# Expert stage of an attention and mixture-of-experts kernel: VectorE turns x from slot 4 and h from slot 5 on, and its turn of h goes first

## The chip, the cores and the metric

The kernel runs on one core of one Trainium2 chip. The metric is the device time of one execution in microseconds. Before the change it is 828.74 us, the median of three runs (827.8 to 831.38).

## The reference

```
scores = q k^T / 8, masked by blocks of 64, softmax, times v     # 8 batches, 8 heads, 576 x 64
x = attention output, 4608 tokens x 512
expert_idx = argmax of the cosine of x and 8 expert vectors; gate_w = its softmax value
for e in 8 experts:
    h = relu(x[mask] @ w1[e])                 # 512 -> 1024
    out[mask] = gate_w[mask] * (h @ w2[e])    # 1024 -> 512
```

All of it is float32. Each token goes to one expert only, and how many each expert gets depends on the data.

## The kernel before

The attention stage writes each token's row of x into a DRAM table, sorted by expert. The expert stage, about the second half of the time, then works in *slots* of 128 tokens of one expert. A table on the chip (`tab`) says for each slot which rows it takes, and whether it is the first of its expert. Two slots are done early, while the attention stage ends; the others are numbered from 0, and each has a `first(g)` and a `second(g)` in the program.

**One slot.** Layer 1 (`layer1`, in `first`) multiplies x by w1, layer 2 (`layer2`, in `second`) multiplies h by w2. To keep float32 precision each operand is split into a high part and a low part, and each product is three TensorE matmuls (`mm3`, L932): 24 matmuls per layer and slot. The high part is a cast on ScalarE, the low part a subtraction on VectorE. TensorE contracts over partitions, so x and h must first be *turned* (transposed).

**Two ways to turn.** TensorE can do it: `xt` turns x with four transposes (L911), `ht` turns h with eight (L963). Or VectorE does it: its transpose works inside blocks of 32 x 32 (`turned`, L860), and the blocks are brought to their places by DMA. For x this is done while it is fetched: `fetch` issues four DMAs in place of one (L851 in place of L848). For h it needs a trip through DRAM: `h_store` (L882, on ScalarE's DMA queue, two halves) writes the relu's result, `h_load` (L890, on GpSimd's queue, four DMAs into the single buffer `hq`) reads it back by blocks, `h_turn` is the pair of VectorE transposes into PSUM, and `h_in` makes the high parts (ScalarE, L869) and low parts (VectorE, L867).

**What sets which way.** `TURN` is the first slot whose h VectorE turns, `XTURN` the number from which x goes to VectorE (x of slot `XTURN + 1` is the first). `LAG` is `TURN - 2`: up to slot LAG layer 2 of slot g - 1 follows layer 1 of slot g; slot LAG + 1 has no layer 2; from then on layer 2 of slot g - 2 follows layer 1 of slot g, so that the trip of h has the time of a slot.

**Weights.** w1 and w2 of an expert are loaded raw (`load_raw`, SyncE's DMA queue, into a single buffer per layer) and split into the half of a ring that the expert before last used: per layer four pieces of 128 x 1024, each a cast on ScalarE (L714) and a subtraction on VectorE (L718). The pieces are placed by the slot G at which an expert begins, two at a time, and stand under an `If` on the slot's flag (`next_weights`): layer 1's in `second(G - 1)` and `first(G)`; layer 2's in `first(G + 1)` and `second(G + 1)`, or one slot later once the lag is two (`seconds`). When pieces are split, the raw weights of the next expert but one are loaded into their place. In slots where no expert begins, the branch skips them.

**Order.** The program is written out by hand, and every engine runs its own instructions in that order. So the lines of `second` are the order on VectorE and on ScalarE: x's turn and its parts, then pieces of weights, then (before the change) the turn of h; `h_load` and `fetch` on GpSimd's queue; layer 2; at the end the parts of h. `last` finishes the last slots and is not touched.

Of the kernel before, what the change touches and what calls it, by code (L numbers as in the profile page):

```python
# [34 lines left out]
def kernel(  # L35
# [755 lines left out]
        nc.vector.tensor_copy(tab.rearrange("p f s -> p (f s)"), tp[0:1, 0:NFL * n])  # L791

    AHEAD = 4
    TURN = 12
    LAG = TURN - 2
    XTURN = 6

    def rotate(pool, name, n, shape, dt):
        sets[name] = [pool.tile(shape, dt, name=f"{name}{i}") for i in range(n)]
# [18 lines left out]
    def next_weights(g, i, cs=range(NPC)):  # L818
        if g >= NSLOT:
            return  # L820
        sl = slots[g]
        if g == 0:
            for c in cs:
                split_hi(i, c, 1)
                split_lo(i, c, 1)
            load_raw(i, 2, cs)
            return
        body = sl["body", i]
        for en, fn in (("act", split_hi), ("dve", split_lo)):
            with tc.If(sl["to", en] != 0):  # L830
                to = sl["to", en] & 1
                for c in cs:
                    ins = fn(i, c, to)
                    for en2, c2, o in body:
                        if en2 != en and c2 != c:
                            tc.declare_no_dep(ins.ins, o.ins, reason="other columns of the ring")
                    body.append((en, c, ins))
        with tc.If(sl["first_sp"] != 0):
            load_raw(i, sl["en2"], cs)

    def fetch(g, eng=nc.gpsimd, et=mybir.EngineType.Pool):
        slots[g]["xg"] = xg = take("xg")
        slots[g]["gate"] = take("gate")
        w = DM // GQ
        r = nc.values_load(tab[0:1, 5, g:g + 1], min_val=0, max_val=(E * RE - 1) * P, engines=[et])
        rows = xs[bass.ds(r, P), :]
        if g <= XTURN:
            eng.dma_start(xg, rows[:, 0:DM])  # L848
        else:
            for q_ in range(GQ):  # L850
                eng.dma_start(xg[32 * q_:32 * q_ + 32].rearrange("j (g w) -> j g w", g=GQ),  # L851
                                    rows[:, q_ * w:(q_ + 1) * w].rearrange("(g j) w -> j g w", g=GQ))
        eng.dma_start(slots[g]["gate"], rows[:, DM:DM + TW])
# [4 lines left out]
    def turned(rows, cs, nk):  # L858
        out = take("px")
        nc.vector.transpose(out.rearrange("p (g c j) -> p g c j", g=GQ, j=32),  # L860
                            rows.rearrange("p (g i c) -> p g c i", g=GQ, c=nk)[:, :, cs, :])
        return out.rearrange("p (g c j) -> p c g j", g=GQ, j=32)
# [8 lines left out]
    def x_turn(g):  # L871
        slots[g]["xt"] = turned(slots[g]["xg"], slice(0, NC1), NC1)

    def x_in(g):
        slots[g]["xT"] = take("xh"), take("xl")
        part(0, *slots[g]["xT"], slots[g]["xt"])

    def x_low(g):
        part(1, *slots[g]["xT"], slots[g]["xt"])

    def h_store(g, f):
        nc.scalar.dma_start(hrows[g % 2][f // 512], slots[g]["h"][:, f:f + 512])  # L882

    def h_load(g):

        slots[g]["hq"] = hq = take("hq")
        w = DF // GQ
        for q_ in range(GQ):
            rows = hrows[g % 2][q_ // 2]
            nc.gpsimd.dma_start(hq[32 * q_:32 * q_ + 32].rearrange("j (g x) -> j g x", g=GQ),  # L890
                                rows[:, q_ % 2 * w:(q_ % 2 + 1) * w].rearrange("(g j) x -> j g x", g=GQ))

    def h_turn(g):
        slots[g]["ht"] = [turned(slots[g]["hq"], slice(f, f + 4), NF) for f in range(0, NF, 4)]

    def h_in(g, us=(0, 1)):
        if 0 in us:
            slots[g]["hT"] = take("hh"), take("hl")
        hh, hl = slots[g]["hT"]
        for u in us:  # L900
            for w in range(2):
                part(w, hh[:, 4 * u:4 * u + 4], hl[:, 4 * u:4 * u + 4], slots[g]["ht"][u])

    def xt(g, px=None):
        xt_copy(g, xt_pe(g, px))
# [36 lines left out]
    def layer1(g, out=True):  # L942
# [4 lines left out]
        for f in range(0, DF, 512):  # L947
# [3 lines left out]
            slots[g]["h"] = h  # L951
            if out and g >= TURN:
                h_store(g, f)

    def ht(g, fs=(0, 4), pts=None):
        for f in fs:
            ht_copy(g, f, ht_pe(g, f, None if pts is None else pts[f // 4]))
# [28 lines left out]
    def layer2(g, cs=None, y=None):  # L986
        if cs is None or 0 in cs:
            slots[g]["py"] = take("py")
        py = slots[g]["py"]
        mm3(g, 1, py, slots[g]["hT"], DM, NF, 0, cs)  # L990
        if cs is None or NF - 1 in cs:
            give(g, py, slots[g]["gate"][:, 0:1], token(slots[g]["gate"]), y)
# [52 lines left out]
    for u in range(EARLY):  # L1045
        g = len(slots)
# [121 lines left out]
    def seconds(g):  # L1168
        return g - 1 if g < LAG + 2 else g - 2
# [15 lines left out]
    def second(g):  # L1185

        if g >= NU - 1:
            for f in range(0, DF, 512):
                h_store(g, f)
        if g < XTURN:  # L1190
            xt(g + 1)
        if g >= XTURN - 1 and g + 2 < NSLOT:
            x_turn(g + 2)
            x_in(g + 2)
            x_low(g + 2)
        if g != LAG + 2:
            next_weights(seconds(g), 1, (2, 3))
        if g == 1:
            next_weights(1, 0)
        next_weights(g + 1, 0, (0, 1))  # L1200
        if g > TURN:
            h_turn(g - 1)
        if g >= TURN:
            h_load(g)
        if g <= LAG:
            layer2(g - 1)
        elif g > LAG + 1:
            layer2(g - 2, y=slots[g + 2]["xg"] if g + 2 < NSLOT else None)
        if LAG + 1 < g <= TURN:
            ht(g - 1)  # L1210
        if g + AHEAD < NSLOT:
            fetch(g + AHEAD)
        if g > TURN:
            h_in(g - 1)
# [15 lines left out]
    def rest(g):  # L1230

        if g + 1 == NSLOT:
            last(g)
            return
        used = nc.values_load(tab[0:1, 3, g + 1:g + 2], min_val=0, max_val=1)
        with tc.If(used != 0) as c:  # L1236
            second(g)
            first(g + 1)
            rest(g + 1)
        with c.Else():  # L1240
            last(g)

    for g in range(1, NU):
        first(g)
        if g < NU - 1:
            second(g)
# [49 lines left out]
```

## Time and profile before

| | |
|---|---|
| median of three runs | 828.74 us (827.8 to 831.38) |
| the profiled execution | 831.03 us, span 829.4 us |
| granted clock of TensorE, mean | 0.982 |
| TensorE busy | 800.4 us, 97% of the span |
| VectorE, ScalarE, GpSimd busy | 529.9, 409.9, 421.4 us |
| moved by DMA | 121.17 MB, mean 146 GB/s |

The expert stage proper, where `first` and `second` alternate, goes from about 422 us of the span to its end. An instruction's row gives its line, its engine and the tiles that it writes and reads. A bracket tells how long the engine was idle before it and what ended that: another engine's result, a DMA's landing, or the engine's own queue of branches (a name with a q).

### The profile page before, as it was taken

How to read it: one execution, taken by the hardware profiler on the slowest of the kernel's cores; microseconds unless marked ns; L12 is line 12 of the kernel's file. 1: busy time of each engine (PE TensorE's matmuls, PEld its weight loads, DVE VectorE, ACT ScalarE, POOL GpSimd, SP SyncE). 2: the span in 40 equal slices, each digit the busy share in tenths (PEclk: the TensorE clock that was granted, in tenths of full speed). 3: DMA queues.
4: the chain of work that ended last, by engine and by line, in shares of the span. 5: the costliest groups of instructions: out<-in, count | busy, mean ns of one | idle time of the engine just before them, and what ended most of it. 6: DMA issues, size and time to landing. Idle time of an engine off the chain costs nothing. (4 is left out here: it accounts for less than half of the span.)

```text
span 829.4 us, 21361 instructions
## 1 busy us (share of the span) xinstructions
PE 800.4 (97%) x6575; PEld 630.6 (76%) x6575; DVE 529.9 (64%) x981; ACT 409.9 (49%) x733; POOL 421.4 (51%) x554
## 2 busy tenths in 40 slices
PE   6999999999999999987999999999999999999996
PEld 3777777777777777765778888888888888888875
DVE  5677878787878787846843346655766554665441
ACT  2444646575746565665544446554544333543332
POOL 4366665756565656552421322335565555455551
PEclk7899999999999999988999999999999999999999
DMA  4766454545444454363475425767868544454441
GB/s 65 145 153 140 88 140 76 140 86 145 90 120 100 109 119 90 104 239 129 152 286 171 155 66 166 242 194 205 248 219 259 155 137 149 130 154 154 150 136 42
DMA packets 147124, 121.17 MB, mean 146 GB/s; under 512 B 123102, under 2 KB 123422, under 8 KB 145436
## 3 DMA queue, kind: packets, MB, share of 16 engines
q1 hardware_dynamic: 122752, 62.33, 29.9%
q0 software_dynamic: 17584, 44.98, 18.2%
q10 hardware_dynamic: 6636, 12.09, 4.0%
q8 instruction: 63, 1.03, 0.6%
q14 instruction: 89, 0.73, 0.3%
HBM read 84.90 MB, written 35.27 MB: 145 GB/s over the span
## 5 line engine op out<-in xcount | busy, mean ns | idle before, releaser
L365 ACT ACTIVATE pT<-psp 128x576 f32<-128x576 f32 (+2 forms) x192 | 112.5, 614 | 44.7 <-PE psp L235 43.8
L347 POOL TENSOR_TENSOR pS<-pT 128x896 f32<-128x896 f32 (+1 forms) x32 | 66.6, 2080 | 104.8 <-ACT pT L365 104.8
L235 PE MATMUL psp<-hi 64*128 64x64 f32 (+6 forms) x768 | 115.1, 336 | 3.9 <-DVE nmx L316 1.7
L316 DVE TENSOR_REDUCE nmx<-psp 128x2 f32<-128x1024 f32 (+3 forms) x128 | 103.3, 823 | 20.4 <-PE psp L235 15.8
L932 PE MATMUL py<-ring_h,hh 128*128 (+1 forms) x288 | 112.7, 391 | 0.4 <-issue 0.4
L932 PE MATMUL py<-ring_h,hl 128*128 (+1 forms) x288 | 112.3, 390 | 0.0
L932 PE MATMUL py<-ring_l,hh 128*128 (+1 forms) x288 | 112.1, 389 | 0.0
L932 PE MATMUL ph<-ring_h,xh 128*128 x280 | 110.0, 393 | 0.4 <-issue 0.4
L383 PE MATMUL psb<-pT,vo 128*64 128x448 f32 (+4 forms) x768 | 105.3, 411 | 4.5 <-DVE lgh L431 4.1
L932 PE MATMUL ph<-ring_h,xl 128*128 x280 | 109.1, 390 | 0.0
L932 PE MATMUL ph<-ring_l,xh 128*128 x280 | 109.0, 389 | 0.0
L235 PEld LDWEIGHTS psp<-hi 64*128 64x128 f32 (+1 forms) x768 | 71.7, 184 | 42.0 <-DVE lo L301 9.8
L890 POOL DMA_DIRECT2D hq<-hrows x92 | 50.3, 553 | 99.2 <-DVE px L860 87.3
L347 POOL TENSOR_TENSOR pS<-pS,pT 128x640 f32<-128x640 f32 (+3 forms) x96 | 96.0, 1000 | 9.0 <-ACT pT L365 1.7
L718 DVE TENSOR_TENSOR ring_l<-raw,ring_h 128x1024 f32 (+1 forms) x64 | 78.1, 1233 | 17.7 <-ACT ring_h L714 11.2
L950 ACT ACTIVATE h<-ph 128x512 f32<-128x512 f32 x70 | 41.8, 597 | 83.5 <-PE ph L932 74.2
L383 PEld LDWEIGHTS psb<-pT,vo 128*64 128x64 f32 x768 | 49.2, 142 | 42.9 <-issue 25.6
L399 ACT COPY so<-psb 128x896 f32<-128x896 f32 x32 | 29.0, 907 | 103.7 <-PE psb L397 103.7
L301 DVE TENSOR_TENSOR lo<-psp,hi 128x640 fp32r<-128x640 f32 x64 | 48.5, 758 | 34.5 <-ACT hi L299 32.0
L714 ACT CAST ring_h<-raw 128x1024 f32 (+1 forms) x64 | 66.5, 1053 | 7.2 <-ACTq L830 4.2
L860 DVE STREAM_TRANSPOSE px<-hq 128x512 f32<-128x512 f32 x46 | 50.7, 1146 | 19.6 <-DMA hq<-hrows 7.9
L932 PEld LDWEIGHTS py<-ring_h,hh 128*128 128x128 f32 x288 | 54.1, 188 | 11.8 <-issue 0.8
(243 smaller groups left out, 1654.5 us busy)
## 6 DMA issues: line engine op xcount, KB each, us to landing
raw<-in_moe_w_dram SPq DMA_DIRECT2D x40, 512.0 KB
raw<-in_moe_w_dram SPq DMA_DIRECT2D x12, 1024.0 KB
hrows<-h ACTq DMA_DIRECT2D x46, 256.0 KB
hq<-hrows POOLq DMA_DIRECT2D x92, 128.0 KB, 3.1
nat<-in_q_dram SPq DMA_DIRECT2D x64, 144.0 KB
nat<-in_k_dram SPq DMA_DIRECT2D x64, 144.0 KB
vo<-in_v_dram SPq DMA_DIRECT2D x64, 128.0 KB
xg<-xs POOLq DMA_DIRECT2D x64, 64.0 KB, 3.2
```

Source lines behind the costliest of these rows:

```text
L235: nc.tensor.matmul(out(hh), lhsT(hd[hh]), rhs(hd[hh]), start=start, stop=stop)
L301: nc.vector.tensor_tensor(lo_[i][:, :, cs], src, hi_[i][:, :, cs].bitcast(F32), op=ALU.subtract)
L316: nc.vector.tensor_reduce(m[:, :, u], mx[:, :, 0:P * u], axis=AX.X, op=ALU.max, negate=True)
L347: eng.tensor_tensor(o, pT[0:r, hs, P:S] if t == 1 else o, pT[0:r, hs, off[t]:off[t] + w], op=ALU.add)
L365: nc.scalar.activation(pT[0:r, :, o:o + c1 - c0], st[0:r, :, x:x + c1 - c0], AF.Exp, scale=scale)
L383: nc.tensor.matmul(ob[hh * D:(hh + 1) * D, c0:c1], a[:, t, hh, :], pTs[0][:, hh, o:o + c1 - c0], start=(t == 0), stop=(c0 == OB or t == NJ ...
L714: return nc.scalar.copy(piece(ring_h, to, c, half), raw[i][:, c * CW:(c + 1) * CW])
L718: return eng.tensor_tensor(piece(ring_l, to, c, half), raw[i][:, c * CW:(c + 1) * CW], piece(ring_h, to, c, half).bitcast(F32), op=ALU.sub ...
L860: nc.vector.transpose(out.rearrange("p (g c j) -> p g c j", g=GQ, j=32), rows.rearrange("p (g i c) -> p g c i", g=GQ, c=nk)[:, :, cs, :])
L890: nc.gpsimd.dma_start(hq[32 * q_:32 * q_ + 32].rearrange("j (g x) -> j g x", g=GQ), rows[:, q_ % 2 * w:(q_ % 2 + 1) * w].rearrange("(g j) ...
L932: m = nc.tensor.matmul(out, a[:, c, :], w, start=(c == 0 and w is wh and a is sh), stop=(c == nk - 1 and a is sl_))
L950: nc.scalar.activation(h[:, f:f + 512], ph, AF.Relu)
```

## The change

`TURN` goes from 12 to 5 and `XTURN` from 6 to 3; with TURN, LAG goes from 10 to 3. In `second`, the call of `h_turn` moves from behind the weights' pieces to the front, ahead of x's turn.

```diff
     AHEAD = 4
-    TURN = 12
+    TURN = 5
     LAG = TURN - 2
-    XTURN = 6
+    XTURN = 3
...
         if g >= NU - 1:
             for f in range(0, DF, 512):
                 h_store(g, f)
+        if g > TURN:
+            h_turn(g - 1)
         if g < XTURN:
             xt(g + 1)
         if g >= XTURN - 1 and g + 2 < NSLOT:
...
         if g == 1:
             next_weights(1, 0)
         next_weights(g + 1, 0, (0, 1))
-        if g > TURN:
-            h_turn(g - 1)
         if g >= TURN:
             h_load(g)
```

VectorE's instructions in the second half of slot 13, before the change (px are PSUM tiles of turned blocks, xg a slot's x, hq the h that was loaded back, ring_h and ring_l the weights' parts, 6409 layer 2's and 6178 layer 1's):

```order
L860 STREAM_TRANSPOSE px_6687<-xg_6415 128x512
...
L867 TENSOR_TENSOR xl_6189<-px_6687,xh_6187 128x512
...
L718 TENSOR_TENSOR ring_l_6409<-raw_6179,ring_h_6408 128x1024
...
L718 TENSOR_TENSOR ring_l_6178<-raw_109,ring_h_6177 128x1024
...
L860 STREAM_TRANSPOSE px_6685<-hq_6413 128x512
L860 STREAM_TRANSPOSE px_6686<-hq_6413 128x512
L867 TENSOR_TENSOR hl_6253<-px_6685,hh_6252 128x512
L867 TENSOR_TENSOR hl_6253<-px_6686,hh_6252 128x512
```

The same place with the change, again VectorE in the second half of slot 13:

```order
L860 STREAM_TRANSPOSE px_6690<-hq_6413 128x512
L860 STREAM_TRANSPOSE px_6688<-hq_6413 128x512
L860 STREAM_TRANSPOSE px_6689<-xg_6415 128x512
...
L867 TENSOR_TENSOR xl_6189<-px_6689,xh_6187 128x512
...
L718 TENSOR_TENSOR ring_l_6409<-raw_6179,ring_h_6408 128x1024
...
L718 TENSOR_TENSOR ring_l_6178<-raw_109,ring_h_6177 128x1024
...
L867 TENSOR_TENSOR hl_6253<-px_6690,hh_6252 128x512
L867 TENSOR_TENSOR hl_6253<-px_6688,hh_6252 128x512
```

The pair of turns of hq has moved ahead of x's turn, its low part and the pieces of both rings; the low parts of h stay last. From slot 6 on VectorE has this order in every slot.

TensorE where slot 7 begins, before the change (py is layer 2's sum, ph layer 1's):

```order
L932 MATMUL py_6688<-ring_h_6408,hl_6253 128x512
L963 MATMUL px_6687<-ident,h_6250 128x128 x4
L963 MATMUL px_6685<-ident,h_6250 128x128 x4
L943 TENSOR_LOAD tab
...
L932 MATMUL ph_6683<-ring_h_6177,xh_6187 128x512
```

TensorE at the same place with the change:

```order
L932 MATMUL py_6692<-ring_h_6408,hl_6253 128x512
L943 TENSOR_LOAD tab
L943 ISA x2
L932 ISA
L932 MATMUL ph_6686<-ring_h_6177,xh_6187 128x512
```

The eight transposes of h between the two layers are gone.

## Rows read from the trace of the kernel before

In a timeline the columns are start, length, engine, line, operation, tiles written and read, number, and in brackets the idle time ahead with what ended it.

**Rows 1.** The page's first part, TensorE's line: busy us (share), instructions.

```profile
PE 800.4 (97%) x6575; PEld 630.6 (76%) x6575; DVE 529.9 (64%) x981; ACT 409.9 (49%) x733; POOL 421.4 (51%) x554
```

**Rows 2.** Two stretches: us, PE, PEld, DVE, ACT, POOL busy, clock, DMA, GB/s.

```profile
492.00:560.00 68.00, 68.00 (x325) 57.10 (x324) 41.14 (x42) 38.87 (x54) 22.50 (x35) 1.00 0.63 197
574.00:642.00 68.00, 68.00 (x302) 56.31 (x301) 47.34 (x49) 33.44 (x49) 38.89 (x62) 1.00 0.76 239
```

**Rows 3.** TensorE's timeline: layer starts in slots 5, 6, 7, 13, 14, 15, 17.

```profile
471.15 0.48 PE L932 MATMUL ph<-ring_h,xh 128*128 x1
...
483.50 0.48 PE L932 MATMUL ph<-ring_h,xh 128*128 x1
...
495.31 0.48 PE L932 MATMUL ph<-ring_h,xh 128*128 x1
...
565.37 0.39 PE L932 MATMUL py<-ring_h,hh 128*128 x1
...
570.81 0.39 PE L932 MATMUL ph<-ring_h,xh 128*128 x1
...
581.69 0.39 PE L932 MATMUL ph<-ring_h,xh 128*128 x1
...
608.89 0.39 PE L932 MATMUL py<-ring_h,hh 128*128 x1
```

**Rows 4.** VectorE's timeline around slot 14.

```profile
572.21 1.29 DVE L867 TENSOR_TENSOR hl<-px,hh 128x512 fp32r<-128x512 f32 x2 [1.50 <-ACT hh L869]
574.02 2.56 DVE L718 TENSOR_TENSOR ring_l<-raw,ring_h 128x1024 f32 x2 [0.53 <-ACT ring_h L714]
576.91 1.11 DVE L860 STREAM_TRANSPOSE px<-xg 128x512 f32<-128x512 f32 x1 [0.33 <-DMA ex<-xs]
578.67 0.69 DVE L867 TENSOR_TENSOR xl<-px,xh 128x512 fp32r<-128x512 f32 x1 [0.65 <-ACT xh L869]
579.62 2.55 DVE L718 TENSOR_TENSOR ring_l<-raw,ring_h 128x1024 f32 x2 [0.25 <-ACT ring_h L714]
582.87 2.20 DVE L860 STREAM_TRANSPOSE px<-hq 128x512 f32<-128x512 f32 x2 [0.69 <-DMA gate<-xs]
584.96 1.45 DVE L867 TENSOR_TENSOR hl<-px,hh 128x512 fp32r<-128x512 f32 x2
587.23 1.10 DVE L860 STREAM_TRANSPOSE px<-ex 128x512 f32<-128x512 f32 x1 [0.81 <-DVEq L830]
```

**Rows 5.** ScalarE's timeline at the start of slot 14.

```profile
571.01 0.69 ACT L979 ACTIVATE xg<-py,gate 128x512 f32<-128x512 f32 x1 [3.86 <-PE py L932]
571.60 1.07 ACT L869 CAST hh<-px 128x512 fp32r<-128x512 f32 x2
572.54 2.16 ACT L714 CAST ring_h<-raw 128x1024 f32 x2
```

**Rows 6.** Stores and loads of h, in order of time, from four engines' timelines.

```profile
555.88 0.33 ACTq L882 DMA_DIRECT2D hrows<-h  x1
...
560.12 2.19 POOL L890 DMA_DIRECT2D hq<-hrows  x4 [6.54 <-DMA hrows<-h]
...
599.18 1.65 SPq L136 DMA_DIRECT2D raw<-in_moe_w_dram  x2
...
600.41 0.36 ACTq L882 DMA_DIRECT2D hrows<-h  x1
...
609.66 1.09 POOL L890 DMA_DIRECT2D hq<-hrows  x2 [2.71 <-DMA hrows<-h]
...
613.53 2.22 DVE L860 STREAM_TRANSPOSE px<-hq 128x512 f32<-128x512 f32 x2 [2.13 <-DMA hq<-hrows]
```

**Rows 7.** Splits on VectorE, 492 to 560 us: busy, mean ns | idle.

```profile
L718 DVE TENSOR_TENSOR ring_l<-raw,ring_h 128x1024 f32 x20 | 24.4, 1226 | 5.8 <-ACT ring_h L714 2.2 <-DMA raw<-in_moe_w_dram 1.9 <-DVE ring_l L718 0.5
...
514.93 5.01 DVE L718 TENSOR_TENSOR ring_l<-raw,ring_h 128x1024 f32 x4 [0.25 <-ACT ring_h L714]
```

**Rows 8.** Tile hq, the h loaded back: time from issue to landing.

```profile
DMA to landing us min/median/max: 2.8/3.1/4.9
```

## The prediction

> **What bounds the kernel now.** I read the page first. TensorE is busy for 97% of the span [rows 1]. A share over the whole span says little about one stage, so the next view was the busy time by stage: in both stretches of the expert stage TensorE works 68.00 of 68.00 us [rows 2]. It waits for nothing there, so whatever is taken off TensorE shortens the kernel, and whatever makes it wait lengthens it, one for one. The third view was TensorE's timeline, where one reads the step from slot to slot; the last were the timelines of VectorE, ScalarE and GpSimd in single slots, to see how late the turned h may come.
>
> **What goes from TensorE.** The start of layer 1 in slots 5, 6, 7, 14 and 15 stands in [rows 3]. A slot with both turns on TensorE takes 483.50 - 471.15 = 12.35 us, one that turns h alone 495.31 - 483.50 = 11.81, one with none 581.69 - 570.81 = 10.88. So a turn of x costs 0.54 us and a turn of h 0.93. Slots 5 to 11 lose the turn of h and slots 4 to 6 that of x: 7 x 0.93 + 3 x 0.54 = 8.1 us. The slot in which layer 2 is skipped to gain the longer lag moves from 11 to 4; the number of layers stays, so this costs nothing. ScalarE's and VectorE's high and low parts of h and x stay as many as before.
>
> **What is added, and what hides it.** Per slot VectorE gets a pair of h turns, 2.20 us, and in three slots an x turn, 1.11 us [rows 4]. In 492 to 560 us it was busy 41 of 68 us [rows 2], so seven pairs (15.4 us) fit as a mean. ScalarE gets two stores of h per slot, GpSimd four loads of 0.55 us, and x of slots 4 to 6 comes in four pieces in place of one; GpSimd was busy 22.5 of 68 us there, and it waits for layer 2's result anyway. I cost these issues at nothing. If that cover went, the whole of four issues, 2.2 us, would come into the trip of h priced below.
>
> **What becomes tight.** h of slot g-1 must be cut into its parts before layer 2 of that slot starts. I count from the moment when TensorE enters the second half of slot g (its layer 1 is done); 10.9 us later it needs the high parts, and after two matmuls (5.44 us for 24, so 0.45) the first low part. The budget is 11.3 us plus whatever TensorE already lost in this slot. Let the pair of h turns start at L. Then the changed order puts on VectorE: the pair 2.2, the turn of x 1.1, the high part of x on ScalarE 0.65, its low part 0.7, then the weights' low parts, then the low parts of h [rows 4]. ScalarE is in order too, and its high part of x stands ahead of layer 2's result (0.6) and of the high parts of h (0.6 each) [rows 5]. So the wait for h is now also a wait for x and weights, on both engines. From L to the end of the first low part of h:
> - no weights in the half: 2.2 + 1.1 + 0.6 + 0.6 + 0.6 + 0.7 = 5.8 us;
> - a pair of weight pieces: 2.2 + 1.1 + 0.65 + 0.7 + 0.25 + 2.55 + 0.7 (branch) + 0.7 = 8.9 us;
> - two pairs, by the row with four pieces, 5.01 us [rows 7]: 10.6 us.
> Another 0.6 us later VectorE is free. From there to the next pair of turns it needs 0.8 us (584.96 + 1.45 to 587.23), with a pair of pieces in the next first half 3.4 (572.21 + 1.29 to 576.91) [rows 4], with two pairs 3.4 + 2.8 = 6.2.
>
> **The trip of h through memory.** Here I bound from both sides. Quiet: a store issued at 555.88 let the load go at 560.12, 4.24 us. Behind weights: the store of 600.41 was issued beside two loads of raw weights (from 599.18 on), and the load of its half started only at 609.66, 9.25 us [rows 6]. The turn behind it began at 613.53, 4.6 us after the second half of slot 17 (608.89 [rows 3]). So L is 4.6 where the slot before split a pair in its first half. The other bound is from the load of 560.12: its last issue starts at 561.8 and lands a median 3.1 us later [rows 8], at 564.9, 0.5 us ahead of slot 13's second half (565.37 [rows 3]); that step still had a turn of h on TensorE, so without it L is 0.4. Before the change such lateness cost nothing, since x and the weights went ahead of the turn.
>
> On this the Trainium skill has a rule ("DMA: Bandwidth & Descriptors", section "Queues, rings and completion order"): a DMA engine goes round the queues that hold work and drains a whole packet from one before it turns to the next. By it a store would share with every load in flight, not only with one issued just ahead of it. The rows above agree for one store. By the rows the sum is the one below, by the rule it is nearer to the slow rival.
>
> **The sum, slot by slot.** VectorE's 20 pieces in 492 to 560 us [rows 7], those of [rows 4] and the loads of 599.18 [rows 6] fit experts that begin at slots 7, 9, 12 and 16. With the longer lag the second-layer pieces come one slot later, so slots 6 to 18 get (pairs in first half, second half): 6 (0,1), 7 (1,0), 8 (0,1), 9 (2,1), 10 (0,0), 11 (1,2), 12 (1,0), 13 (0,0), 14 (1,1), 15 (0,1), 16 (1,0), 17 (0,0), 18 (1,1).
> - Slot 8: after slot 7's pair L is 4.6; I add 1.8, the step from the median landing of 3.1 us to the longest, 4.9 [rows 8], as this stretch had 197 GB/s already [rows 2] and gets 1 MB of h in every 10.9 us on top, some 96 GB/s, above the 239 of the stretch from which the 4.6 is. 6.4 + 8.9 = 15.3, over the budget by 4.0.
> - Slot 9: VectorE ends slot 8 at 15.9; + 6.2 - 10.9 gives L = 11.2; + 8.9 = 20.1 against 11.3 + 4.0: 4.8.
> - Slot 10: its step is 10.9 + 4.0, so L = 20.7 + 0.8 - 14.9 = 6.6, and 12.4 against 11.3 + 4.8. Slot 11: L = 13.0 + 3.4 - 15.7 = 0.7, 11.3 against 11.3. Slots 12 and 13, with L = 4.6: 10.4. No wait.
> - Slot 14: L = 11.0 + 3.4 - 10.9 = 3.5, 12.4: 1.1. Slot 15: L = 4.6, 13.5 against 12.4: 1.1. Slots 16 to 19 end inside their budgets.
> Together 11.0 us of new waits against 8.1 saved: +2.9 us. The profiled execution took 831.03 us (span 829.4 and what lies around it), 2.3 above the median of the runs, 828.74. So 833.9 for a like execution and 831.6 on the runs' scale.
>
> **Rivals.** *The trips stay quiet.* If the loads of weights, which the new order also moves, miss the stores, L is 0.4 wherever the trip sets it. Slot 8 then ends at 9.9, and only slot 9 is over: L = 9.9 + 6.2 - 10.9 = 5.2, 14.1, a wait of 2.8. Total -8.1 + 2.8 = -5.3: 823.4 us. For it: the seven turns fit as a mean, and the store of 555.88 came through in 4.24 us. Against it: the stretch that gets the turns is the one with four experts' weights in it.
>
> *The trips get slower still.* If the load back of h is held up as the store was, by some 4 us more, L becomes 8.6 after each first half with a pair. It decides from L = 11.3 - 5.8 = 5.5 in a slot without splits and from 2.4 in one with a pair. By the same steps slots 8, 9, 12, 14, 15, 18 and 19 are over by 6.2, 4.8, 3.1, 2.0, 4.2, 0.9 and 2.2: 23.4, so +15.3: 844.0 us. For it: the 9.25 us row, and that each wait of VectorE now holds the splits back, and with them later loads. Against it: each wait of TensorE gives the memory time.
>
> *The removed turns were free.* Then neither gain nor more than the waits: 840. The fixed steps of [rows 3] and TensorE's 68.00 of 68.00 speak against it; I give it almost nothing.
>
> **Chances.** Forecast 0.43 (own range 826.5 to 837), quiet trips 0.26, slower trips 0.23, the rest in between. A measurement can tell about 0.5%, 4.1 us. Below 824.6 lie most of the quiet case and a little of the forecast's, 0.26; above 832.9 lie the slow one and the upper part of the forecast's range, 0.41; between, 0.33. The range goes from 822.0, a little under the quiet case, to 843.0, just short of the slow one.
>
> **What would show it.** TensorE's turns of h fall from 12 slots to 5 ahead of the last slots, and the step of a free slot from 11.81 to 10.88. The waits, if I am right, stand before layer 2's matmuls, ended by VectorE's low part or ScalarE's high part of h, mostly 10 to 30 us after slot 7, and VectorE waits for the h that was loaded. If TensorE is dense in slots 8 to 16, the quiet case holds. If it waits in slots 12, 15, 18 and 19 too, the slow one does. I am wrong altogether if the waits are of another kind: a bank of PSUM not free, raw weights not landed, or x late for layer 1.

## The result, and the profile after

The changed kernel takes 841.17 us (median of 4 runs, 841.08 to 843.02), the kernel before in the same comparison 829.83 (4 runs): ratio 1.014, 95% interval 1.0117 to 1.0163. The profiled execution took 841.15 us, its span is 839.5 (before 829.4). This and the other ratios below leave out executions over 1.5% above their kernel's fastest, of which only number 3 (four of ten) and the kernel before beside numbers 1 to 4 (three of 31) had any.

TensorE's share and two stretches, which answer to [rows 1] and [rows 2], in the same columns:

```profile
PE 799.4 (95%) x6507; PEld 624.3 (74%) x6507; DVE 544.4 (65%) x998; ACT 407.9 (49%) x733; POOL 442.5 (53%) x591
```

```profile
492.00:560.00 68.00, 62.34 (x260) 49.90 (x259) 45.67 (x48) 33.89 (x48) 32.10 (x52) 0.95 0.74 233
574.00:642.00 68.00, 64.17 (x269) 50.65 (x268) 45.42 (x48) 32.03 (x47) 36.56 (x61) 0.97 0.70 214
...
660.00:814.00 154.00, 154.00 (x681) 127.55 (x680) 83.02 (x94) 57.85 (x96) 87.88 (x145) 1.00 0.48 150
541.00:550.00 9.00, 8.32 (x25) 6.58 (x26) 6.89 (x7) 4.71 (x8) 4.96 (x8) 0.64 0.67 194
540.70:541.60 0.90, 0.00 (x0) 0.00 (x0) 0.00 (x0) 0.90 (x3) 0.32 (x2) 0.50 0.85 250
```

TensorE was dense in both stretches before; now it loses 5.7 and 3.8 us in them, and its clock is below 1.00. Behind 660 us it is dense again. The loss lies at layer 2 in the second halves of slots 10 to 19; the prediction counts such a wait to the slot before, in whose second half that h is turned, and so does this text: slots 9 to 18. What TensorE waited for there (engine, line, releaser: us, times, longest):

```profile
PE py L932 <- ACT hh L869: 8.5, 6, 3.7
PE py L932 <- DVE hl L867: 1.4, 4, 0.7
```

Only the two parts of h, always ahead of layer 2. TensorE's timeline, first where slots 7 to 9 begin (to be compared with [rows 3]), then at the longest wait and at one behind which the clock stays up:

```profile
487.09 0.39 PE L932 MATMUL ph<-ring_h,xh 128*128 x1
...
497.97 0.39 PE L932 MATMUL ph<-ring_h,xh 128*128 x1
...
508.85 0.39 PE L932 MATMUL ph<-ring_h,xh 128*128 x1
...
541.68 0.79 PE L932 MATMUL py<-ring_h,hh 128*128 x1 [3.67 <-ACT hh L869]
...
542.70 0.63 PE L932 MATMUL py<-ring_h,hl 128*128 x1
543.12 0.63 PE L932 MATMUL py<-ring_h,hh 128*128 x1
...
628.27 0.50 PE L932 MATMUL py<-ring_h,hh 128*128 x1 [0.84 <-ACT hh L869]
628.61 0.40 PE L932 MATMUL py<-ring_l,hh 128*128 x1
```

A slot without a wait now takes 10.88 us: the turns are gone as foreseen. The wait of 3.67 us has a tail: up to 547.5 us the matmuls come every 0.43 us instead of every 0.23. The row of 541 to 550 us above gives the granted clock there as 0.64; TensorE has it at the lower of its two levels, 1.2 GHz, for 6.83 us, and for 3.41 us again behind the wait of 2.01 us at 581. The 6.83 us begin at 540.67, a us before the wait ends: in the row of 540.70 to 541.60 the clock is 0.50 and TensorE has no matmul. Where the clock stays at 1.00, the first matmuls behind a wait still come every 0.33 to 0.39 us (628.27 to 628.61).

Why the h of slot 9 was late in slot 10 is read from four engines. VectorE:

```profile
504.92 2.18 DVE L860 STREAM_TRANSPOSE px<-hq 128x512 f32<-128x512 f32 x2 [4.26 <-DMA hq<-hrows]
507.01 1.06 DVE L860 STREAM_TRANSPOSE px<-ex 128x512 f32<-128x512 f32 x1
...
519.05 2.18 DVE L860 STREAM_TRANSPOSE px<-hq 128x512 f32<-128x512 f32 x2
...
536.19 2.17 DVE L860 STREAM_TRANSPOSE px<-hq 128x512 f32<-128x512 f32 x2 [8.33 <-DMA ex<-xs]
538.28 1.04 DVE L860 STREAM_TRANSPOSE px<-xg 128x512 f32<-128x512 f32 x1
```

ScalarE:

```profile
503.61 0.60 ACT L950 ACTIVATE h<-ph 128x512 f32<-128x512 f32 x1 [2.12 <-PE ph L932]
504.24 0.33 ACTq L882 DMA_DIRECT2D hrows<-h  x1
508.10 0.59 ACT L869 CAST xh<-px 128x512 fp32r<-128x512 f32 x1 [3.89 <-DVE px L860]
...
512.66 4.18 ACT L714 CAST ring_h<-raw 128x1024 f32 x4
516.74 0.59 ACT L950 ACTIVATE h<-ph 128x512 f32<-128x512 f32 x1
517.37 0.34 ACTq L882 DMA_DIRECT2D hrows<-h  x1
...
518.38 0.45 ACTq L882 DMA_DIRECT2D hrows<-h  x1
...
539.36 0.59 ACT L869 CAST xh<-px 128x512 fp32r<-128x512 f32 x1 [10.60 <-DVE px L860]
540.46 0.69 ACT L979 ACTIVATE xg<-py,gate 128x512 f32<-128x512 f32 x1 [0.52 <-ACTq L830]
541.05 1.06 ACT L869 CAST hh<-px 128x512 fp32r<-128x512 f32 x2
```

GpSimd, which loads h back:

```profile
525.76 1.10 POOL L890 DMA_DIRECT2D hq<-hrows  x2 [9.32 <-DMA hrows<-h]
527.68 1.09 POOL L890 DMA_DIRECT2D hq<-hrows  x2 [0.83 <-DMA hrows<-h]
```

SyncE, which loads the raw weights:

```profile
511.55 8.05 SPq L136 DMA_DIRECT2D raw<-in_moe_w_dram  x5
...
526.48 0.33 SPq L136 DMA_DIRECT2D raw<-in_moe_w_dram  x1
```

Read it as a circle. At 504.92 the h of slot 7 comes to VectorE, which has waited 4.26 us for it. The turn of x stands behind it, and ScalarE's cast of x waits for that (3.89 us). So ScalarE is late for its next work in order, two weight pieces, y, the high parts of h and four more pieces, and the relu of slot 9 comes at 516.74 and 517.75: layer 1 of slot 9 had ended at 514.45, and the second store leaves at 518.38, 3.9 us later, where a free ScalarE needs 0.67 (503.57 to 504.24). Not all of that is the cast's: in number 5 below, where x is not held, the same store still leaves 1.85 us after layer 1, behind the four pieces. The stores now also meet five weight loads; GpSimd gets the landed halves 8.4 and 9.3 us after the issues (quiet it was 4.24 [rows 6]). The load back is late as well: its last part, issued at 528.23 after the weight load of 526.48, lands after 7.7 us, at 535.97. So the h of slot 9 is turned only at 536.19, after 8.33 us of waiting (the releaser named there is a neighbour in time; the wait is for hq), and x's cast is held 10.60 us, and with it the next relu. In the 16 slots from 470 to 653 us the second store leaves 3.0 us after the end of layer 1 as a mean, 7.9 at most (the issue's row less the end of the last ph row); before, 1.05 and 2.2.

Over the whole stage the load back is no slower than before in the median (2.8 us, before 3.1 [rows 8]), but its longest has gone from 4.9 to 7.7, and that one is slot 10's. Tile hq's line, over the stage and for 527 to 529 us alone:

```profile
DMA to landing us min/median/max: 2.5/2.8/7.7
...
DMA to landing us min/median/max: 7.7/7.7/7.7
```

### The profile page after: what moved, and what is told of

It reads as the page before. It is cut to its first block, busy times and chain, and to the rows that moved or that the text cites. A ratio compares the mean times of both kernels' runs of the same rounds, so it can differ in the third digit from the quotient of the medians.

```text
span 839.5 us, 21306 instructions
## 1 busy us (share of the span) xinstructions
PE 799.4 (95%) x6507; PEld 624.3 (74%) x6507; DVE 544.4 (65%) x998; ACT 407.9 (49%) x733; POOL 442.5 (53%) x591
## 5 line engine op out<-in xcount | busy, mean ns | idle before, releaser
L890 POOL DMA_DIRECT2D hq<-hrows x120 | 65.8, 553 | 118.1 <-DMA hrows<-h 57.8
L932 PE MATMUL py<-ring_h,hh 128*128 (+1 forms) x288 | 115.0, 399 | 8.5 <-ACT hh L869 8.5
L316 DVE TENSOR_REDUCE nmx<-psp 128x2 f32<-128x1024 f32 (+3 forms) x128 | 103.2, 823 | 21.6 <-PE psp L235 18.7
L932 PE MATMUL py<-ring_h,hl 128*128 (+1 forms) x288 | 114.6, 398 | 1.4 <-DVE hl L867 1.4
L932 PE MATMUL py<-ring_l,hh 128*128 (+1 forms) x288 | 113.9, 396 | 0.0
L235 PEld LDWEIGHTS psp<-hi 64*128 64x128 f32 (+1 forms) x768 | 72.3, 185 | 42.8 <-DVE lo L301 10.1
L860 DVE STREAM_TRANSPOSE px<-hq 128x512 f32<-128x512 f32 x60 | 65.9, 1144 | 56.6 <-DMA hq<-hrows 33.4
L718 DVE TENSOR_TENSOR ring_l<-raw,ring_h 128x1024 f32 (+1 forms) x64 | 78.1, 1234 | 17.3 <-ACT ring_h L714 12.4
L950 ACT ACTIVATE h<-ph 128x512 f32<-128x512 f32 x70 | 41.8, 598 | 69.7 <-PE ph L932 44.4
L867 DVE TENSOR_TENSOR hl<-px,hh 128x512 fp32r<-128x512 f32 x60 | 38.7, 685 | 55.9 <-ACT hh L869 55.0
```

The source lines that it names most:

```text
L235: nc.tensor.matmul(out(hh), lhsT(hd[hh]), rhs(hd[hh]), start=start, stop=stop)
L316: nc.vector.tensor_reduce(m[:, :, u], mx[:, :, 0:P * u], axis=AX.X, op=ALU.max, negate=True)
L718: return eng.tensor_tensor(piece(ring_l, to, c, half), raw[i][:, c * CW:(c + 1) * CW], piece(ring_h, to, c, half).bitcast(F32), op=ALU.sub ...
L867: nc.vector.tensor_tensor(lo, src, hi.bitcast(F32), op=ALU.subtract)
L932: m = nc.tensor.matmul(out, a[:, c, :], w, start=(c == 0 and w is wh and a is sh), stop=(c == nk - 1 and a is sl_))
L950: nc.scalar.activation(h[:, f:f + 512], ph, AF.Relu)
```

## The experiments

The measure beside the ratio is the *stage of experts* in each profiled execution: from the start of layer 1's first matmul in slot 1 to the end of TensorE's last (an expectation below calls it slot 0's; layer 1 of slot 0 is done earlier, beside the two early slots). Of the changed kernel, first and last rows:

```profile
422.30 0.50 PE L932 MATMUL ph<-ring_h,xh 128*128 x1 [0.41 <-issue]
...
832.16 0.39 PE L932 MATMUL py<-ring_h,hl 128*128 x1
```

that is 832.55 - 422.30 = 410.25 us; before, 401.05 (421.81 to 822.86). Each stage is that of one execution; the two of the changed kernel differ by 0.9 us. Numbers 1 to 4, 10 and 11 ran on two chips on which the kernel before takes 872 us; in their traces TensorE's clock up to 420 us is 0.92 to 0.93 as a mean, where the trace of before has 0.97. Their ratios are to those 872 us, and in the stage of experts the clock is 1.00 there too where nothing waits. "Held" is the time for which ScalarE's cast of x (from the eighth on: or y) waited for VectorE's turn of x in some 210 us from slot 6 on; "half" the time at half clock inside the stage.

| kernel | ratio to before (95%) | stage, us | held, us | half, us |
|---|---|---|---|---|
| before | 1 | 401.05 | 7.7 | 0 |
| changed kernel | 1.014 (1.0117 to 1.0163) | 410.25 | 69.7 | 10.24 |
| the same again | 1.0118 (1.0100 to 1.0136) | 409.39 | 64.5 | 3.41 |
| 1 numbers only | 0.9985 (0.9947 to 1.0024) | 399.55 | 13.2 | 3.41 |
| 2 order only | 1.0062 (1.0022 to 1.0102) | 407.80 | 37.5 | 3.41 |
| 3 x only | 0.9941 (0.9887 to 0.9994) | 399.44 | 5.8 | 0 |
| 4 small loads | 0.9907 (0.9867 to 0.9948) | 392.65 | 25.2 | 0 |
| 5 x first | 1.0005 (0.9994 to 1.0017) | 400.04 | 21.6 | 3.41 |
| 6 pieces first | 1.0123 (1.0106 to 1.0140) | 408.69 | 69.9 | 6.83 |
| 7 between | 0.9994 (0.9981 to 1.0008) | 399.76 | 14.7 | 3.41 |
| 8 cast late | 1.0094 (1.0077 to 1.0111) | 409.59 | 0 (y: 56.4) | 10.24 |
| 9 loads behind | 1.0157 (1.0140 to 1.0174) | 413.52 | 12.3 | 6.83 |
| 10 y apart | 0.9982 (0.9951 to 1.0013) | 401.99 | 0 (y: 0) | 3.41 |
| 11 TURN 10 | 0.9968 (0.9941 to 0.9994) | 398.26 | 5.7 | 0 |

**1. Numbers only.** The order of before, with the new TURN and XTURN:

```diff
-        if g > TURN:
-            h_turn(g - 1)
         if g < XTURN:
...
         next_weights(g + 1, 0, (0, 1))
+        if g > TURN:
+            h_turn(g - 1)
```

> The kernel with the change, but with the turn of h in its old place behind x's turn and the weights' low parts. Theory (the trip of h through memory is late where weights are loaded, and the new order makes x and the weights wait for it too): behind the turn only the parts of h are left, 1.1 + 0.6 + 0.7 = 2.4 us to the first low part, so a trip may end 8.9 us into the slot; of the trips in the trace after, 11.0 us in slot 10 and 8.5 in slot 13, only the first is over, by about 2 us, and VectorE alone costs some 2 us in slots 9 and 11. About 4 to 5 us of waits against 8.1 saved: 826 to 828 us, faster than before by 2 to 4. Rival (VectorE has too much to do in slots 8 to 12, in whatever order): the waits stay near those after, 838 to 842 us.

The stage takes 399.55 us, 10.7 under the changed kernel and 1.5 under before, a little less than the theory's 2 to 4. So the order costs most of the loss, but 6.6 of the 8.1 us saved go all the same: one wait of 2.96 us, 3.41 us of half clock from about its end on, smaller waits.

**2. Order only.** The new order with TURN 12 and XTURN 6. 

> The kernel before with the turn of h moved ahead, and the numbers 12 and 6 as before. Theory: slots 13 to 19 wait as in the trace after, where slots 14, 16, 18 and 19 lost 2.0, 0.2, 0.8 and 0.8 us and TensorE ran at half its clock for 3.4 us: 3 to 6 us slower than before, 833 to 836 us. Rival (the order costs nothing, since h is loaded by the time it is turned): within 1 us of before.

+6.75 us in the stage, a little over the theory's 3 to 6, and +0.6% in the ratio, inside it. Here the waits are at a few slots from 15 on:

```profile
PE py L932 <- ACT hh L869: 3.1, 2, 2.1
...
PE py L932 <- DVE hl L867: 0.6, 2, 0.3
```

**3. x only.** The kernel before with XTURN 3. 

> The kernel before with XTURN at 3 alone, so that x of slots 4 to 6 is turned by VectorE and nothing else changes. Theory: three turns of x leave TensorE, 3 x 0.54 = 1.6 us, and no h goes through memory earlier: 828.2 us, 0.998 of before. Rival (x in four pieces comes late, or VectorE is late): no change or slower.

The stage is 1.61 us shorter; three turns of x at 0.54 are 1.62. The ratio in the table is lower than the expected 0.998; the means of all executions of both kernels, 868.8 and 871.2 us, give 0.997, and the ten of this kernel spread over 14.9 us. The stage is the better measure here.

**4. Small loads.** The changed kernel, but the raw loads of later experts bring 128 columns of each piece (of two pieces for layer 2); most of those weights are then old ones.

```diff
-            load_raw(i, sl["en2"], cs)
+            load_raw(i, sl["en2"], cs, 128)
```

> The kernel with the change, but the weights of the experts from the third on are loaded only in part: 128 of every 1024 columns (of every 2048 where two pieces share one load), so that the rest of these weights is stale; all splits and matmuls are done as before. Theory (the loads of weights make the trip of h late): nearly all waits go but one of 1 to 3 us in slot 9, where VectorE has three pairs of pieces; 823 to 825 us, 16 to 18 under the kernel with the change. Rival (VectorE's and ScalarE's own work is too much): still 837 us or more.

The windows of the same columns as above:

```profile
487.00:700.00 213.00, 213.00 (x952) 176.60 (x951) 142.29 (x152) 105.12 (x155) 116.78 (x190) 1.00 0.47 147
```

TensorE is dense, with the changed order, all of its splits, stores and issues; the one wait that the theory left in slot 9 did not come either. The stage is 8.40 us under before: the saving of 8.1, paid out. So neither VectorE's extra work nor the issues cost anything; the waits need the traffic of weights. What that traffic lengthens is the trip of h: by the records of the DMA packets a store takes 1.5 to 3.0 us from its issue to its last packet here, and 1.5 to 8.0 with the change. It does not say how that comes to hurt so much in one order and less in another.

**The changed kernel again, and 5 and 6.** The order of the three things in the second half of a slot: h's turn (h), x's turn with its parts (x), the weights' pieces (p). The changed kernel has h, x, p and number 1 has x, p, h. Number 5 is x, h, p; number 6 is p, h, x. The edit of number 5:

```diff
-        if g > TURN:
-            h_turn(g - 1)
         if g < XTURN:
             xt(g + 1)
...
             x_low(g + 2)
+        if g > TURN:
+            h_turn(g - 1)
         if g != LAG + 2:
```

> The changed kernel as it is, beside the kernel before on the same chip, so that the runs with other orders have their own base. The stage of experts (from the first matmul of slot 0's layer 1 to TensorE's last) took 401.05 us in the trace of before and 410.25 in that of the changed kernel. If waits and clock come from the kernel's own order and transfers, the stage takes 409 to 412 us here too, with stretches of half clock behind waits of over 2 us, and the ratio is 1.009 to 1.014. If the drops of the clock were an accident of that one execution: about 405.

> Changed kernel, but x's turn and its parts go ahead of h's turn; the weights' pieces stay behind it. Theory (h's late trip holds VectorE, x's turn stands behind it, ScalarE's cast of x waits for that, and the relu and the store of the next h stand behind this cast on ScalarE, so that each late h makes the next one leave late): without x in the hold the stores leave at once behind their relu, and the stage of experts takes 396 to 402 us, 8 to 14 under 410.25. Rival (what hurts is that the weights' pieces stand behind h's turn, and with them the parts of h at the end and the weight loads): 407 to 411.

> Changed kernel, but the weights' pieces go ahead of h's turn; x's turn and its parts stay behind it. Theory (the cast of x that waits behind h's turn holds the relu and the store of the next h): h's turn is late still in the slots with pieces, x's cast too, and the stage of experts takes 403 to 409 us. Rival (the pieces behind h's turn are what hurts): as with all of it ahead, 398 to 401 us.

The repeat gives 409.39 us; its waits lie partly elsewhere (1.56, 1.86, 2.25, 1.5 and 1.92 us are the longest) and only one is followed by half clock, but the sum is nearly the same. Number 5 takes 9.4 us off this repeat, its base on the same chip, with the move of one call, as the theory expected (10.2 off the first execution); number 6, with the pieces out of the way of h and x behind it, takes off 0.7, no more than the two executions of the changed kernel differ, and in that case the rival was wrong by 8 us. What costs is that x stands behind h. ScalarE's waits, first of the changed kernel, then of number 6, then of number 5:

```profile
ACT xh L869 <- DVE px L860: 69.7, 14, 10.6
```

```profile
ACT xh L869 <- DVE px L860: 69.9, 15, 6.9
```

```profile
ACT xh L869 <- DVE px L860: 21.6, 12, 3.8
```

Number 6 was to come out between 403 and 409 and is at the upper end.

**7. Between.** x, layer 2's pieces, h, layer 1's pieces. 

> Changed kernel, with h's turn between the two pairs of pieces: x's turn, layer 2's pieces, h's turn, layer 1's pieces. With all four pieces ahead of h's turn the stage took 399.55 us, with one wait of 2.96 us behind four pieces (5.0 us on VectorE) and 3.41 us of half clock after it. Theory: the turn is then behind two pieces at most (2.5 us less), x is out of the hold, that wait falls under 1 us and the clock stays: 394 to 398 us. Rival (loads of h behind weight loads decide, wherever the turn stands): 398 to 403.

399.76 us, the rival's range. The wait behind the slot with four pieces stays (2.7 us, ended by the low part of h, with 3.41 us of half clock from about its end on): the low parts of h stand behind all four pieces wherever the turn stands.

**8. Cast late.** VectorE's order of the changed kernel; the cast of x goes behind the next relus.

```diff
             x_turn(g + 2)
-            x_in(g + 2)
-            x_low(g + 2)
...
         layer1(g, out=g < NU - 1)
+        if g >= XTURN and g + 1 < NSLOT:
+            x_in(g + 1)
+            x_low(g + 1)
```

> Changed kernel with VectorE's order as it is (h's turn, x's turn, pieces), but ScalarE's cast of x, and the low part of x with it, moved out of the second half of the slot to behind the two relus of the next layer 1. Theory (the cast of x behind the late turn of h holds relu and store of the next h on ScalarE): the stores leave at once behind their relu, and the stage of experts takes 398 to 404 us, where the changed kernel takes 409.4 and 410.3 and the one with x's turn ahead of h's 400.0. Rival (x's turn behind h's hurts on VectorE itself, by what it puts off there): 407 to 411, with the wait in the cast's new place.

A miss: 409.59 us, although the second stores leave earlier than with the change, 2.0 us after layer 1 as a mean in place of 3.0. ScalarE's timeline shows why:

```profile
527.76 0.59 ACT L869 CAST xh<-px 128x512 fp32r<-128x512 f32 x1 [0.40 <-DMA hq<-hrows]
538.48 0.69 ACT L979 ACTIVATE xg<-py,gate 128x512 f32<-128x512 f32 x1 [10.13 <-DVEq L830]
539.07 1.07 ACT L869 CAST hh<-px 128x512 fp32r<-128x512 f32 x2
```

The cast is out of the way, and ScalarE stands for 10.13 us at the next thing, y. `layer2` writes y into xg, the buffer of the x that VectorE has still to turn, so y waits for the same turn. Over the stretch:

```profile
ACT xg L979 <- DVEq L830: 29.9, 6, 10.1
ACT ex L979 <- DVEq L830: 26.5, 5, 7.3
```

The trace names VectorE's branch queue as releaser; that it is the turn of x follows from the code, and number 10 tries it.

**9. Loads behind.** The order of 7, and from slot 5 on the weight loads of a slot wait for its store of h: they are issued behind `h_load`, each group behind a small load that reads the stored h.

```diff
+        with tc.If(sl["first_sp"] != 0):
+            if row is not None:
+                nc.sync.dma_start(tick[0:1, 16 * k:16 * k + 16], row[0:1, 0:16])
+            load_raw(i, sl["en2"], cs)
```

> Order of x's turn, layer 2's pieces, h's turn, layer 1's pieces (399.8 us), and from slot 5 on SyncE's weight loads wait: those of a slot go behind one small load that reads the stored h of that slot, so that h's store is on the chip's DRAM before the next weights' transfers begin. Theory (what is left of the waits, some 4 us and 3.4 us of half clock, comes from h's trip behind weight loads): stores take 2 to 4 us each, not 6 to 10, the waits of layer 2 go, and the stage takes 392 to 396 us, some 1% under before. Rival (the transfers need this time, so that weights come late instead): layer 1 or 2 waits for the parts of weights, 399 us or more.

Neither: 413.52 us, worse than all, and the waits are for the parts of h, not for weights. By the DMA packets a store still took up to 8.8 us from its issue to its last packet. And the edit puts the weights beside the load back of h, which is issued as soon as the store has landed: its median from 480 to 690 us is 4.7 us, where the changed kernel has 2.9 in that stretch. Tile hq's line:

```profile
DMA to landing us min/median/max: 2.7/4.7/10.7
```

The store itself was held, too. ScalarE:

```profile
529.92 0.34 ACTq L898 DMA_DIRECT2D hrows<-h  x1
530.36 0.60 ACT L966 ACTIVATE h<-ph 128x512 f32<-128x512 f32 x1 [1.12 <-DMA tick<-hrows]
534.67 0.33 ACTq L898 DMA_DIRECT2D hrows<-h  x1
```

The store at 534.67 left 3.7 us after its relu, and the relu's row names a small load as releaser. That the store waited for small loads which stood in SyncE's queue behind weights is likely and not shown. So this run does not decide whether weights that miss both the store and the load back would help; that stays open.

**10. Cast late and y apart.** Number 8, with y in two buffers of its own:

```diff
-                rotate(mq, "y", 1, [P, DM], F32)
+                rotate(mq, "y", 2, [P, DM], F32)
...
-            layer2(g - 2, y=slots[g + 2]["xg"] if g + 2 < NSLOT else None)
+            layer2(g - 2)
```

> As the kernel with the late cast of x (VectorE's order of the changed kernel; stage of experts 409.59 us), but y of layer 2 goes into two buffers of its own, where it was written into the buffer of the x that VectorE turns behind h. With the late cast alone ScalarE stood 10.13 us at y instead of 10.60 at the cast: y had to wait until x was turned. Theory, mended by that (what holds ScalarE ahead of the next relu is whatever needs the turn of x, the cast or y): with both out of the way the relu follows layer 1 by under 2 us, the store with it, and the stage takes 399 to 405 us. Rival (VectorE's own lateness decides, whoever waits for it on ScalarE; the high parts of h hold the relu all the same): 406 to 411.

401.99 us, inside the theory's range, 7.6 under number 8. ScalarE's waits in the same slots:

```profile
ACT y L979 <- PE py L932: 48.8, 16, 5.7
ACT h L950 <- PE ph L932: 33.9, 21, 2.1
ACT hh L869 <- DVE px L860: 5.3, 7, 2.9
```

It waits for TensorE's results, as it should, and for VectorE 5.3 us in all. The second store leaves 1.1 us after layer 1 as a mean. VectorE still has its order of h, x, p and still waits 6.00 us once for a late h, so x behind h does little harm on VectorE itself (the stage is 2.0 us over number 5's); the harm was done on ScalarE. Two things change with it: the next store leaves early, and the high parts of h no longer stand behind a cast and a y that wait for x's turn. From the start of h's turn to its first low part it is 5.7 us as a mean here, 7.3 with the change. Number 6 has the same 5.6 us, but its second stores leave 2.7 us after layer 1, and its stage is 6.7 us longer: so the shorter way behind the turn is not by itself what was gained. How the 8 us divide between the two is not shown; number 8 has a little of both (6.1 and 2.0 us) and gains nothing.

**11. TURN 10, XTURN 3, order of before.** 

> Kernel before with two numbers changed and its own order: x from slot 4 on (XTURN 3), h from slot 10 on (TURN 10). With XTURN 3 alone the stage took 399.44 us; two turns of h less on TensorE are 1.87 us. With TURN 5 in this order the waits were at the layer 2 that uses the h of slots 8 to 10; if they grow from one late h to the next, the first h here, slot 10's, meets nobody late ahead of it and there are no waits: 397.6 us, 3.5 under before, ratio 0.996. Rival (the slot with four pieces of weights is too full for h's turn by itself): a wait of 1 to 3 us and half clock behind it, 400 to 403 us, ratio 0.999 to 1.002.

398.26 us, 2.8 under before, no half clock and no wait over 0.6 us; ratio 0.9968. Of the kernels that compute everything it has the shortest stage; number 3 has a lower ratio in the table (0.9941), the two intervals overlap, and over all executions the two come to the same 0.997. Its stretch with the most traffic, in the columns of the windows above:

```profile
540.00:700.00 160.00, 159.89 (x717) 132.33 (x717) 103.74 (x108) 80.86 (x116) 81.28 (x132) 1.00 0.71 225
```

The same slot with four pieces that cost 2.96 us in number 1 costs nothing here, where h is not already late from the slot ahead: the rival, that the slot is too full by itself, falls.

## Why the prediction came out as it did

The side was right and the range held, by some luck: 841.17 us lies outside the forecast's own range (826.5 to 837), and the outer range reached that far only because of the slow rival. The point, 831.6, was 9.6 us too low.

- **The saving, 8.1 us: right.** Slots of 10.88 us, and -8.40 us in the stage once no wait is left (4), -1.61 for x alone (3).
- **Work and issues cost nothing: right** (4).
- **From the turn to the parts, 5.8, 8.9 and 10.6 us: right.** From 536.19, without pieces, the first low part of h ended 6.1 us later; from 519.05, with one pair, 8.2; from 546.40, with two, 10.4. (The sum of 10.6 leaves out the 0.7 for the branch that the one of 8.9 has.)
- **The waits: the sum nearly right by luck, the places wrong.** 11.0 us were predicted, 9.9 came (9.5 more than before). Slots 8 and 9 were to have 8.8 of it and had 1.25; slots 10 and 13 were to have none and had 3.7 and 2.0. The waits lie 28 to 143 us behind slot 7, not mostly 10 to 30. The turn of slot 10 started 11.0 us after layer 1, not 6.6, that of slot 13 8.5, not 4.6. The step that failed is the trip of h: it was priced from the issue of the store, and the store was taken to leave as soon as layer 1 is done. The working had the cause in hand, "the wait for h is now also a wait for x and weights, on both engines", but followed ScalarE only to the high parts of h, and not on to the next relu and store, which stand behind them. So each late h was to cost its own slot, while it in fact made the next h leave late. Numbers 5, 6 and 10 show that this hold on ScalarE is what costs. The same trip was also priced too low at its end: the load back was taken at 3.1 us, in slot 8 at 4.9, and in slot 10 it took 7.7.
- **"Lengthens it, one for one": wrong, and this is the missing sum.** The stage grew by 9.2 us, so 17.3 us were lost against 8.1 saved, with waits of only 9.5. Of the 10.24 us at half clock 1.0 lies inside the wait; the other 9.2 are 4.6 us of work. The rest, 3.2 us, is what is left over; the first matmuls behind each wait, which come every 0.33 to 0.39 us in place of 0.23, have a part of it. In the repeat 11.1 us of waits cost 16.4. A further 0.9 us of the span's 10.1 lie outside the stage.
- **The rival with slower trips, 844.0, came nearer by its number, and by half of its mechanism.** It had the load back slower by some 4 us wherever weights were split; the load's median went from 3.1 to 2.8 us, but in slot 10, the one with the longest wait, it took 7.7, 4.6 more. What the rival did not have is the store, late in leaving; and number 5, with loads back of up to 7.3 us and stores as slow, loses 9.4 us less, so slow trips alone do not make the loss. The rule of the Trainium skill ("DMA: Bandwidth & Descriptors", section "Queues, rings and completion order"), that a DMA engine goes round all queues that hold work, fits the store that was issued at 518.38, without being shown by it: the last of five weight loads had been issued by 519.60, and GpSimd saw the store landed 9.3 us after its issue.

## What to carry to other kernels

If an instruction that may wait is moved forward on an in-order engine, follow the hold through every engine that needs what stands behind it, up to the instruction that starts the next round of the same trip: a loop through a second engine can turn a hidden latency into one that feeds itself. Look at buffers too: a result written into the buffer of an operand not yet read waits with it. And a wait of the engine that bounds costs more than its length, here 1.5 to 1.8 times.

## What was not expected of the hardware

TensorE's clock fell to half behind waits of a few us in a stage that had run at 1.00 throughout: 6.83 us at half about the end of the one of 3.67, 3.41 behind 2.01, and stretches of 3.41 or 6.83 us in every other kernel whose longest wait was 1.9 us or more, in none of those whose longest was 0.6 or less; no kernel lies between. The length of the wait alone does not tell when. In the repeat of the changed kernel it fell behind waits of 1.56 and 0.24 us, and not behind 2.25 and 0.73; the two windows:

```profile
527.00:532.00 5.00, 4.76 (x13) 3.53 (x14) 1.29 (x2) 1.54 (x3) 3.80 (x6) 0.66 0.87 242
555.00:560.00 5.00, 3.54 (x14) 2.63 (x15) 3.96 (x6) 4.08 (x7) 4.70 (x7) 1.00 0.95 276
```
